# Last block of a windowed-attention layer: normalised values written in the row order of the output weights, transposed on the whole array, and a value halo of 128 columns

## The chip, the cores and the metric

The kernel runs on one core of a Trainium2 chip. The metric is the device time of the whole program in microseconds, as the median of several runs. A core has TensorE (PE; its weight loads are listed as PEld), VectorE (DVE), ScalarE (ACT), GpSimd (POOL) and SyncE (SP, which issues nearly all DMAs here). Each engine takes its instructions in the order of the program, and they wait for one another through semaphores. SBUF is the working memory of 128 partitions; PSUM holds what TensorE writes, in eight banks of 512 f32 values per partition.

## The reference

Four layers A, B, A, B act on x of 2048 positions and 512 features, all in bf16, with 32 heads of 16 features; both A layers share their weights, and so do both B layers. Layer B is the one that matters here:

```python
W, dil = 8, 2
qkv = (x @ wqkv).reshape(B, S, 3, H, Dh).transpose(2, 0, 3, 1, 4)
idx = pos[:, None] - (jnp.arange(W) * dil)[None, :]      # 8 positions back, every second one
logits = einsum("bhsd,bhswd->bhsw", q, k at idx) * Dh ** -0.5
attn = softmax(where(idx >= 0, logits, -1e9))
o = einsum("bhsw,bhswd->bhsd", attn, v at idx)
return o.transpose(0, 2, 1, 3).reshape(B, S, D) @ wo
```

Each layer's input is x normalised over its features, and its result is added to x. Layer A is a linear attention with softmax feature maps and has the same outer form.

## The kernel before, in words

The 2048 positions are cut into four blocks of 512 (b = 0 to 3), and each of the four layers runs over the blocks. L counts the pairs of layers, so that (L, b) = (1, 3) is the last block of the last layer B. A stage of a block is a list of steps per engine. The steps of all stages are put in one hand-made order, a long string of thread names (`_ORDER`); which engine copies a PSUM bank out (ACT or DVE) and which slot each tile takes are fixed by three more strings (`_CHOICE`, `_SLOTS`). Nothing is planned while the program runs: the order on each engine is the order of that string. The steps of several blocks are mixed, so that block (1, 2), by the general path, runs side by side with block (1, 3).

All blocks of layer B but the last take the general path: VectorE multiplies queries with shifted keys (`prod`, L1042) and weights with shifted values (`pav`, L1104), and TensorE sums over features or window positions with 0/1 matrices of 32 columns (L1049, L1113). The last block, (1, 3), takes another path, in four methods:

- `s_e1` projects keys and queries with features in partitions, and values with positions in partitions. For the window that reaches back, it also projects the last 64 positions of the block before: `hk` for keys, `hv` (L1192) for values, which makes a PSUM result of 64 partitions from 64 columns of stationary operand. `ehv` copies that to partitions 0 to 63 of plane 2 of a staging tile `Vs`, `vwh` (L1234) writes those 64 rows to a DRAM tile, together with the 512 rows of the block (`vwr`, L1231), and `vrd` (L1242) reads all of it back in 32-row groups with every second position, into the old space of a weight tile (`WA`) and a tile `Vx`. Each head has a 17th column of ones.
- `s_e2` makes scores for one of four tiles t of 128 positions (L1277), exponentials (L1298) and the mask (L1303).
- `s_e3` multiplies with the values (L1321, 32 or 8 columns each) into a PSUM tile `O` of two banks, which holds for each of e = 0 to 7 a run of 4 x 17 values, in 128: c = 0 to 3 and, for head 8c + e, 16 values and the sum of weights. The reciprocals of the sums are made on ACT (`ln`, `rd`, L1337 and L1340) as an f32 tile `r` of 8 x 4 (e by c). `nrm` (L1348, VectorE) multiplies and writes the bf16 tile `oB`, for tile t 512 columns in the order head, feature.
- `s_e4` transposes tile t with TensorE (`pt`, L1365), with matmuls whose moving operand is an identity with permuted columns: partitions hold positions sorted by even and odd, and `ident[:].rearrange("p (r q) -> p q r", r=2)` puts them in order again. ACT copies the PSUM bank to `oBT`, and `s_out` multiplies with the output weights (L542) and adds x (L555 on VectorE, or L545 on TensorE with L552 on ACT).

The output weights `WoB` are stored with rows sorted for both paths: chunk q, partition 32c + h holds row 16h + 4q + c. Before, `pt` makes this order: for each q and c, one matmul takes the 32 columns 4q + c, 4q + c + 16, and so on of `oB` as stationary operand and writes 32 partitions, at column tile 32c of the array.

After the last steps the program tests a flag (L1387 to L1415) that says whether the fast path held; the slow path behind it did not run.

Of the kernel before, what the change touches and what calls it, by code (L numbers as in the profile page):

```python
# [11 lines left out]
ALU = mybir.AluOpType  # L12
# [4 lines left out]
P = 128  # L17
NJ = 16
D = 512
H = 32  # L20
DH = 16
NW = 8
HALO = 14
NB = 4
# [8 lines left out]
DV = DH + 1  # L33
# [103 lines left out]
class _Fast:  # L137
# [1023 lines left out]
    def s_e1(self, L, b):  # L1161
        nc, add = self.nc, self.step
        st = "b1_%d%d" % (L, b)
        T = {}

        def mm(i, c):
            xnT = self.xnT["B%d" % L, b]
            T[i, c] = pp = self.ps()
            for k in range(NB):
                nc.tensor.matmul(pp[:], lhsT=self.WB[:, k, i * D + c * P:i * D + (c + 1) * P], rhs=xnT[:, :, k, :],  # L1170
                                 start=(k == 0), stop=(k == NB - 1))

        def hk():
            xp = self.xnT["B%d" % L, b - 1]
            T["hk"] = pp = self.ps()
            for c in range(NB):
                for k in range(NB):
                    nc.tensor.matmul(pp[:, c * 64:(c + 1) * 64], lhsT=self.WB[:, k, D + c * P:D + (c + 1) * P],
                                     rhs=xp[:, 3, k, 64:128], start=(k == 0), stop=(k == NB - 1))

        def mv(t):
            xnT = self.xnT["B%d" % L, b]
            T[2, t] = pp = self.ps()
            for k in range(NB):
                nc.tensor.matmul(pp[:], lhsT=xnT[:, t, k, :], rhs=self.WB[:, k, 2 * D:3 * D],
                                 start=(k == 0), stop=(k == NB - 1))

        def hv():
            xp = self.xnT["B%d" % L, b - 1]
            T["hv"] = pp = self.ps()  # L1190
            for k in range(NB):
                nc.tensor.matmul(pp[0:64, :], lhsT=xp[:, 3, k, 64:128], rhs=self.WB[:, k, 2 * D:3 * D],  # L1192
                                 start=(k == 0), stop=(k == NB - 1))

        def ehk(dve):
            self.copy(dve, self.kvT[:, 0:4 * 64], T["hk"][:, 0:4 * 64])

        def vs(u):
            if ("Vs", u) not in T:
                T["Vs", u] = self.med([3, H, DV], "Vs")  # L1200
            return T["Vs", u]

        def vones(u):
            nc.gpsimd.memset(vs(u)[:, :, :, DH:DV], 1.0)

        def ev(i, c, dve):
            if i == 2:
                self.copy(dve, vs(c // 2)[:, c % 2, :, 0:DH], T[i, c][:].rearrange("p (h d) -> p h d", d=DH))
                return
            if i == 1:  # L1210
                if (L, b) not in self.K:
                    self.K[L, b] = self.med([NB, TB], "K")
                dst = self.K[L, b]
            else:
                if i not in T:
                    T[i] = self.med([NB, TB], "Qs")
                dst = T[i]
            self.copy(dve, dst[:, c, :], T[i, c][:])

        def ehv(dve):  # L1220
            self.copy(dve, vs(0)[0:64, 2, :, 0:DH], T["hv"][0:64, :].rearrange("p (h d) -> p h d", d=DH))

        def qsc(g, i):
            lo = DH * g
            nc.sync.dma_start(out=self.Qbd[i][lo:lo + DH, :, g % 4, :], in_=T[0][lo:lo + DH, 2 * i:2 * i + 2, :])

        def vwr(u):
            if u == 0:
                self.VD[L, b] = self.dram.tile([64 + TB, H * DV], BF16, name="vd%d%d" % (L, b))
            dst = self.VD[L, b][64 + 256 * u:320 + 256 * u, :].rearrange("(t p) d -> p t d", p=P)  # L1230
            nc.sync.dma_start(out=dst, in_=vs(u)[:, 0:2, :, :].rearrange("p t h d -> p t (h d)"))  # L1231

        def vwh():
            nc.sync.dma_start(out=self.VD[L, b][0:64, :], in_=vs(0)[0:64, 2, :, :].rearrange("p h d -> p (h d)"))  # L1234

        def vrd(r, j0, j1, c):
            a = self.VD[L, b][64 * j0 + r:64 * j0 + r + 1, c * 8 * DV:(c + 1) * 8 * DV]
            n = H * DV
            src = bass.AP(a.tensor, a.offset, [[2 * n, 32], [64 * n, j1 - j0], [1, 8 * DV]])
            d = self.chunk(r, j0)[32 * c:32 * c + 32, c, :]  # L1240
            dst = bass.AP(d.tensor, d.offset, [list(d.ap[0]), [VCH, j1 - j0], [1, 8 * DV]])
            nc.sync.dma_start(out=dst, in_=src)  # L1242

        add(st + "h", "PE", hk)
        self.flex(st + "h", ehk)
        for i in (1, 0):
            for c in range(NB):
                add(st + "qk"[i], "PE", mm, i, c)
                self.flex(st + "qk"[i], ev, i, c)
        for i in range(2):  # L1250
            for g in range(8):
                add(st + "q", "SP", qsc, g, i)
        for u in range(2):
            add(st + "v", "POOL", vones, u)
        add(st + "h", "PE", hv)
        self.flex(st + "h", ehv)
        for t in range(4):
            add(st + "v", "PE", mv, t)
            self.flex(st + "v", ev, 2, t)
            if t % 2:  # L1260
                add(st + "v", "SP", vwr, t // 2)
            if t == 1:
                add(st + "v", "SP", vwh)
        for r, j0, j1 in ((0, 0, 9), (1, 0, 2), (1, 2, 9)):
            for c in range(NB):
                add(st + "v", "SP", vrd, r, j0, j1, c)
# [44 lines left out]
    def s_e3(self, L, b, t):  # L1311
        nc, add = self.nc, self.step
        st = "b3_%d%d" % (L, b)
        T = {}

        def pv(e, r, s, n, pos):
            j = 1 + 2 * t + s - (pos > 0)
            E = self.ET[t if s or not pos else (t - 1) % 4]
            ks = 2 * r + (s if not pos else 1 - s)
            q = 32 * (2 * r + s)  # L1320
            nc.tensor.matmul(T["O"][q:q + n, e, 0:NB * DV], lhsT=E[:, e // 4, ks, e % 4, pos:pos + n],  # L1321
                             rhs=self.chunk(r, j)[:, :, DV * e:DV * (e + 1)],
                             start=(e % 4 == 0 and pos == 0), stop=(pos > 0),
                             tile_position=(0, q), skip_group_check=True)

        def mo():
            T["O"] = self.pp().rearrange("p o (e x) -> p (o e) x", x=P)
            for pos, n in ((0, 32), (32, 8)):
                for e in range(8):
                    for r in range(2):  # L1330
                        for s in range(2):
                            pv(e, r, s, n, pos)

        def ln():
            T["r"] = self.sm([8, NB], "rdB")
            den = T["O"][:, :, 0:NB * DV].rearrange("p e (c d) -> p e c d", d=DV)[:, :, :, DH]
            nc.scalar.activation(out=T["r"][:], in_=den, func=ACT.Ln, bias=self.tiny_t[:, 0:1])  # L1337

        def rd():
            nc.scalar.activation(out=T["r"][:], in_=T["r"][:], func=ACT.Exp, scale=-1.0,  # L1340
                                 accum_out=self.stR[:, 7 + t:8 + t])

        def nrm():
            if (L, b) not in self.oB:
                self.oB[L, b] = self.med([4, D], "oB")
            num = T["O"][:, :, 0:NB * DV].rearrange("p e (c d) -> p e c d", d=DV)[:, :, :, 0:DH]
            out = self.oB[L, b][:, t, :].rearrange("p (c e d) -> p e c d", c=NB, d=DH)
            nc.vector.tensor_tensor(out=out, in0=num, in1=T["r"][:].unsqueeze(3).to_broadcast([P, 8, NB, DH]),  # L1348
                                    op=ALU.mult)

        add(st, "PE", mo)
        add(st, "ACT", ln)
        add(st, "ACT", rd)
        add(st, "DVE", nrm)

    def s_e4(self, L, b):
        nc, add = self.nc, self.step
        st, key = "b4_%d%d" % (L, b), "A%d" % (L + 1)
        U = {}

        def pt(t):
            U[t] = self.ps()
            for q in range(NB):
                for c in range(NB):
                    nc.tensor.matmul(U[t][32 * c:32 * c + 32, q * P:(q + 1) * P],  # L1365
                                     lhsT=self.oB[L, b][:, t, 4 * q + c::DH],
                                     rhs=self.ident[:].rearrange("p (r q) -> p q r", r=2), start=True, stop=True,
                                     tile_position=(0, 32 * c))

        def pe(t, dve):  # L1370
            if (key, b) not in self.oT:
# [145 lines left out]
class _Layout:  # L1517
# [6 lines left out]
    def add(self, name, nelem, nbuf=1):  # L1524
        self.regions[name] = (self.off, nelem, nbuf)
        self.off += nelem * nbuf
        return self
# [569 lines left out]
```

## Time and profile before

| | us |
|---|---|
| median of 3 runs (lowest, highest) | 322.31 (322.30, 322.36) |
| the profiled execution, its own time | 321.75 |
| its span, first to last instruction | 320.0 |
| PE busy | 307.5 |
| DVE busy | 295.9 |
| ACT busy | 274.9 |
| the four L1348 on DVE, together | 2.7 |
| the 64 L1365 on PE, together | 2.8 |
| the four L1192 on PE, together | 1.1 |

The page gives busy times for the whole span; the last 25 us are read from the timeline and from groups by shape. In a group's line stand line, engine, operation, tiles, shapes out and in, and count; behind the bar the busy time in us and the mean of one in ns; and behind the second bar the idle time ahead of them with what ended it. In a timeline's line stand start and length in us from the span's start; several instructions of a kind in a row are one line with a count. PE's matmuls overlap: the length of one, some 380 ns for 512 columns, is not the step from one to the next, some 216 ns.

### The profile page before, as it was taken

To read this page: it belongs to the slowest core of one execution; us is meant where nothing else is said; L and a number is where in the kernel's file an instruction comes from. 1 tells how busy PE (TensorE), PEld (TensorE's weight loads), DVE (VectorE), ACT (ScalarE), POOL (GpSimd) and SP (SyncE) were. 2 spreads that over 40 slices of the span, in tenths; PEclk is the share of its full clock that TensorE was granted. 3 is DMA by queue.
4 is the path that set the end of the run, shared out by engine and by line. 5 is a ranking of instruction groups with operands and counts; after the bars stand their busy time and mean duration, and the time that the engine had idled before them with its cause. 6 is when DMAs were issued, how large, how long until landed. Compare 5 with 4: busy or idle time off the path is not lost. (4 is left out here: it accounts for less than half of the span.)

```text
span 320.0 us, 8889 instructions
## 1 busy us (share of the span) xinstructions
PE 307.5 (96%) x3572; PEld 152.2 (48%) x3572; DVE 295.9 (92%) x458; ACT 274.9 (86%) x638; POOL 47.5 (15%) x64
## 2 busy tenths in 40 slices
PE   7999999899999999999999999879999999999993
PEld 3554456445454444444444455544444444444541
DVE  5999996998999999999999999599997999999993
ACT  4999999999898778999999999799999777698560
POOL 6000000000004121000000000041240744035000
PEclk9999999999999999999999999999999999999999
DMA  6977100005794979948994500014389855567733
GB/s 200 349 193 148 35 2 4 2 18 148 177 160 110 152 134 142 137 83 120 153 132 54 69 0 2 4 39 113 89 171 137 151 120 126 133 159 158 182 137 103
DMA packets 45789, 36.37 MB, mean 114 GB/s; under 512 B 30832, under 2 KB 41136, under 8 KB 45744
## 3 DMA queue, kind: packets, MB, share of 16 engines
q1 hardware_dynamic: 45216, 35.75, 55.8%
q8 instruction: 29, 0.48, 0.7%
q14 instruction: 16, 0.13, 0.2%
q10 hardware_dynamic: 528, 0.02, 0.1%
HBM read 11.13 MB, written 3.25 MB: 45 GB/s over the span
## 5 line engine op out<-in xcount | busy, mean ns | idle before, releaser
L950 PE MATMUL PS<-xnT,WB 128*128 128x512 bf16 x336 | 76.8, 379 | 0.1
L1042 DVE TENSOR_TENSOR prod<-QT,K 128x4096 bf16<-128x4096 bf16 x28 | 63.4, 2286 | 0.5 <-POOL K L976 0.5
L1104 DVE TENSOR_TENSOR pav<-PT,Vg 128x4096 bf16<-128x4096 bf16 (+1 forms) x29 | 62.9, 2215 | 0.2
L950 PEld LDWEIGHTS <-WB 128*128 128x128 bf16 x336 | 37.4, 114 | 36.3 <-issue 3.3
L728 ACT ACTIVATE Eq<-PS 128x512 bf16<-128x512 f32 x64 | 36.3, 619 | 0.0
L621 ACT ACTIVATE Ek<-PS 128x512 bf16<-128x512 f32 x64 | 35.1, 622 | 0.2 <-PE PS L615 0.2
L542 PEld LDWEIGHTS <-oT 128*128 128x128 bf16 x240 | 22.3, 98 | 27.1 <-issue 1.3
L720 PE MATMUL PS<-xnT,WA 128*128 128x512 bf16 x128 | 32.0, 380 | 0.5 <-DVE s L812 0.3
L562 ACT ACTIVATE sqd<-x 128x512 bf16<-128x512 bf16 x48 | 30.0, 635 | 2.2 <-DVE x L555 2.0
L555 DVE SCALAR_TENSOR_TENSOR x<-PS,x 128x512 bf16<-128x512 f32 x47 | 30.9, 684 | 1.0 <-PE PS L542 0.9
L627 PE MATMUL PS<-WA,xnT 128*128 128x512 bf16 x128 | 31.6, 379 | 0.0
L615 PE MATMUL PS<-WA,xnT 128*128 128x512 bf16 x128 | 30.7, 379 | 0.0
L204 ACT CAST oT<-PS 128x512 bf16<-128x512 f32 (+1 forms) x50 | 26.9, 599 | 4.3 <-PE PS L1113 2.6
L542 PE MATMUL PS<-WoA,oT 128*128 128x512 bf16 x128 | 29.8, 380 | 0.0
L542 PE MATMUL PS<-WoB,oT 128*128 128x512 bf16 x112 | 27.3, 379 | 0.0
L204 ACT CAST K<-PS 128x512 bf16<-128x512 f32 x30 | 17.3, 594 | 3.0 <-PE PS L950 1.9
L615 PEld LDWEIGHTS <-xnT 128*128 128x128 bf16 x128 | 12.4, 98 | 14.8 <-issue 0.4
L627 PEld LDWEIGHTS <-xnT 128*128 128x128 bf16 x128 | 12.2, 98 | 14.5 <-issue 0.4
L673 DVE TENSOR_TENSOR Ek<-Ek,rk 128x4096 bf16<-128x4096 bf16 (+1 forms) x10 | 18.6, 1860 | 0.4 <-ACT rk L668 0.4
L720 PEld LDWEIGHTS <-WA 128*128 128x128 bf16 x128 | 11.6, 98 | 14.6 <-issue 1.7
L465 DVE TENSOR_SCALAR xn<-x,rstd,nmr 128x512 bf16<-128x512 bf16 x48 | 17.9, 420 | 0.6
L204 ACT CAST V<-PS 128x512 bf16<-128x512 f32 x26 | 15.2, 596 | 2.6 <-PE PS L950 2.6
(164 smaller groups left out, 501.2 us busy)
## 6 DMA issues: line engine op xcount, KB each, us to landing
Vg<-V SPq DMA_DIRECT2D x112, 131.5 KB, 4.3
Prho<-rd SPq DMA_DIRECT2D x8, 512.0 KB, 5.7
x<-in_A_x_dram SPq DMA_DIRECT2D x3, 512.0 KB, 6.8
WB<-in_B_wqkv_dram SPq DMA_DIRECT2D x3, 512.0 KB, 9.9
out_dram<-x SPq DMA_DIRECT2D x6, 256.0 KB, 2.5
wraw<-in_A_wqkv_dram SPq DMA_DIRECT2D x4, 256.0 KB, 4.3
vd<-Vs SPq DMA_DIRECT2D x2, 272.0 KB, 3.0
x<-in_A_x_dram SPq DMA_DIRECT2D x4, 128.0 KB, 3.6
```

The source lines that it names most:

```text
L204: self.nc.scalar.copy(out=out, in_=in_)
L542: nc.tensor.matmul(y[:], lhsT=lh(t, c), rhs=Wo()[:, c, :], start=(c == 0), stop=(c == NB - 1 and not onpe))
L555: nc.vector.scalar_tensor_tensor(out=xb[:, t, :], in0=T[t][:], scalar=1.0, in1=xb[:, t, :], op0=ALU.mult, op1=ALU.add, **kw)
L562: nc.scalar.activation(out=sqd[:], in_=xb[:, t, :], func=ACT.Square, accum_out=T["ss"][:, t:t + 1])
L615: nc.tensor.matmul(pk[:], lhsT=xnT[:, t, k, :], rhs=self.WA[:, k, D:2 * D], start=(k == 0), stop=(k == NB - 1))
L621: nc.scalar.activation(out=T["E"][:, t, s, :], in_=T["k", t][:], func=ACT.Exp, scale=1.0 - 2.0 * s)
L627: nc.tensor.matmul(pv[:], lhsT=xnT[:, t, k, :], rhs=self.WA[:, k, 2 * D:3 * D], start=(k == 0), stop=(k == NB - 1))
L720: nc.tensor.matmul(pq[:], lhsT=self.WA[:, k, hb * P:(hb + 1) * P], rhs=xnT[:, :, k, :], start=(k == 0), stop=(k == NB - 1))
L728: nc.scalar.activation(out=self.Eq[L, b][s][:, :, hb, :], in_=T[hb][:].rearrange("p (t i) -> p t i", t=4), func=ACT.Exp, scale=1.0 - 2.0 * s)
L950: nc.tensor.matmul(pp[:], lhsT=self.WB[:, k, i * D + c:(i + 1) * D:NB], rhs=xnT[:, :, k, :], start=(k == 0), stop=(k == NB - 1))
L1042: nc.vector.tensor_tensor(out=pr[:], in0=QT[:, c:c + 1, :].to_broadcast([P, NW, TB]), in1=win, op=ALU.mult)
L1104: nc.vector.tensor_tensor(out=pv, in0=PT[:, :, lo:lo + n].unsqueeze(1).to_broadcast([P, NB, 2, n]), in1=vw, op=ALU.mult)
```

## The change

Three edits, all in the path of block (1, 3).

`hv` uses all 128 positions of the last tile of the block before as stationary operand, so that its PSUM result has 128 partitions, of which the last 64 are used. `ehv` copies partitions 64 to 127, to partitions 64 to 127 of `Vs`, and `vwh` writes to DRAM from there.

`nrm` walks its operands in the order feature d, then c, then e. It writes `oB` in the order d, c, e, which is 32d + h, so that columns 128q to 128q + 127 hold the features 4q + c of all heads in the order of the rows of `WoB`. The output is then dense; the PSUM input steps 128 f32 values from one element to the next, and the reciprocals step 4.

`pt` transposes four pieces of 128 dense columns with one matmul of 128 columns each, where it had sixteen of 32. The moving operand, the permuted identity, stays.

The order of steps, the tiles, the slots and the DMAs' sizes stay as they are. On TensorE 48 weight loads and 48 matmuls fall away; the other engines issue as many instructions as before.

```diff
@@ hv
-                nc.tensor.matmul(pp[0:64, :], lhsT=xp[:, 3, k, 64:128], rhs=self.WB[:, k, 2 * D:3 * D],
+                nc.tensor.matmul(pp[:], lhsT=xp[:, 3, k, :], rhs=self.WB[:, k, 2 * D:3 * D],
@@ ehv
-            self.copy(dve, vs(0)[0:64, 2, :, 0:DH], T["hv"][0:64, :].rearrange("p (h d) -> p h d", d=DH))
+            self.copy(dve, vs(0)[64:P, 2, :, 0:DH], T["hv"][64:P, :].rearrange("p (h d) -> p h d", d=DH))
@@ vwh
-            nc.sync.dma_start(out=self.VD[L, b][0:64, :], in_=vs(0)[0:64, 2, :, :].rearrange("p h d -> p (h d)"))
+            nc.sync.dma_start(out=self.VD[L, b][0:64, :], in_=vs(0)[64:P, 2, :, :].rearrange("p h d -> p (h d)"))
@@ nrm
-            num = T["O"][:, :, 0:NB * DV].rearrange("p e (c d) -> p e c d", d=DV)[:, :, :, 0:DH]
-            out = self.oB[L, b][:, t, :].rearrange("p (c e d) -> p e c d", c=NB, d=DH)
-            nc.vector.tensor_tensor(out=out, in0=num, in1=T["r"][:].unsqueeze(3).to_broadcast([P, 8, NB, DH]),
-                                    op=ALU.mult)
+            num = T["O"][:, :, 0:NB * DV].rearrange("p e (c d) -> p d c e", d=DV)[:, 0:DH]
+            out = self.oB[L, b][:, t, :].rearrange("p (d c e) -> p d c e", c=NB, d=DH)
+            rec = T["r"][:].rearrange("p e c -> p c e").unsqueeze(1).to_broadcast([P, DH, NB, 8])
+            nc.vector.tensor_tensor(out=out, in0=num, in1=rec, op=ALU.mult)
@@ pt
-            for q in range(NB):
-                for c in range(NB):
-                    nc.tensor.matmul(U[t][32 * c:32 * c + 32, q * P:(q + 1) * P],
-                                     lhsT=self.oB[L, b][:, t, 4 * q + c::DH],
-                                     rhs=self.ident[:].rearrange("p (r q) -> p q r", r=2), start=True, stop=True,
-                                     tile_position=(0, 32 * c))
+            for c in range(NB):
+                nc.tensor.matmul(U[t][:, c * P:(c + 1) * P], lhsT=self.oB[L, b][:, t, c * P:(c + 1) * P],
+                                 rhs=self.ident[:].rearrange("p (r q) -> p q r", r=2), start=True, stop=True)
```

## The prediction

> **What bounds the kernel where the change acts.** I read the page first, then the busy time by stretches, then the order of VectorE's and TensorE's instructions over the last 25 us, then the groups kept apart by shape. The page names no single bound: TensorE and VectorE are both above 90% of the span.
>
> ```profile
> PE 307.5 (96%) x3572; PEld 152.2 (48%) x3572; DVE 295.9 (92%) x458; ACT 274.9 (86%) x638; POOL 47.5 (15%) x64
> ```
>
> By stretches (busy us of PE, PEld, DVE, ACT, POOL; clock; DMA share), this stretch holds all four normalisations and all four transposes of the last block:
>
> ```profile
> 295.40:308.10 12.70, 12.54 (x258) 6.90 (x257) 12.66 (x18) 8.22 (x21) 0.00 (x0) 1.00 0.60 164
> ```
>
> VectorE is busy for 12.66 of 12.70 us, TensorE for 12.54. VectorE's instructions in order of time (start, length) show where the four L1348 stand:
>
> ```profile
> 295.47 1.28 DVE L1348 TENSOR_TENSOR oB<-PS,rdB 128x512 bf16<-128x512 f32 x2
> 296.67 0.81 DVE L1303 TENSOR_TENSOR et<-et,maskW 128x1280 bf16<-128x1280 bf16 x1
> ...
> 303.01 0.68 DVE L1348 TENSOR_TENSOR oB<-PS,rdB 128x512 bf16<-128x512 f32 x1
> 303.61 0.68 DVE L555 SCALAR_TENSOR_TENSOR x<-PS,x 128x512 bf16<-128x512 f32 x1
> 304.21 2.28 DVE L1104 TENSOR_TENSOR pav<-PT,Vg 128x4096 bf16<-128x4096 bf16 x1
> 306.43 0.69 DVE L1348 TENSOR_TENSOR oB<-PS,rdB 128x512 bf16<-128x512 f32 x1
> ```
>
> Each starts before or as its forerunner ends: there is no hole into which a longer L1348 could grow. Whatever one of them gains or loses, the fourth (306.43 to 307.12) feels four times. TensorE around it:
>
> ```profile
> 306.39 0.67 PE L1365 MATMUL PS<-ident,oB 128*32 128x128 bf16 x16
> 306.88 0.61 PE L1113 MATMUL PS<-pav,indAV 128*32 128x512 bf16 x8
> 307.31 0.67 PE L1365 MATMUL PS<-ident,oB 128*32 128x128 bf16 x16
> 307.91 1.90 PE L542 MATMUL PS<-WoB,oBT 128*128 128x512 bf16 x8
> 309.65 0.17 PE L1396 MATMUL PS<-okb,ones 128*128 128x4 bf16 x1
> 309.67 0.81 PE L542 MATMUL PS<-WoB,oT 128*128 128x512 bf16 x3
> 310.41 0.40 PE L1113 MATMUL PS<-pav,indAV 128*32 128x256 bf16 x8
> 311.29 0.40 PE L1113 MATMUL PS<-pav,indAV 128*32 128x256 bf16 x8 [0.48 <-ACT oT L204]
> ```
>
> The fourth transpose waits for the fourth L1348 (its weight load was idle 0.19 us for it, below). TensorE keeps its order, so L542, the flag matmul, the last L1113 and the closing L542 all queue behind that transpose. So the end is set by VectorE up to 307.12, then by the chain L1365, ACT's copy of oBT, L542, L1113, ACT, L1113, L542.
>
> ```profile
> 307.18 0.53 PEld L1365 LDWEIGHTS <-oB 128*32 128x32 bf16 x16 [0.19 <-DVE oB L1348]
> ```
>
> **Part 1, L1348.** Four instructions, still 512 values each, on the same waits. Each now walks its operands with the head index e innermost: the output becomes dense; the PSUM input steps 128 f32 = 512 bytes per element where it read runs of 16; the reciprocals in SBUF (f32, stored e by c) step 4 f32 = 16 bytes per element where each was held for 16. No row has exactly that. The nearest rows, by shape:
>
> ```profile
> L1348 DVE TENSOR_TENSOR oB<-PS,rdB 128x512 bf16<-128x512 f32 x4 | 2.7, 684 | 0.0
> L555 DVE SCALAR_TENSOR_TENSOR x<-PS,x 128x512 bf16<-128x512 f32 x47 | 30.9, 684 | 1.0 <-PE PS L542 0.9
> L267 DVE TENSOR_REDUCE indAV<-ident 128x32 bf16<-128x128 bf16 x1 | 0.4, 360 | 0.0
> L267 DVE TENSOR_REDUCE indQK<-ident 128x32 bf16<-128x128 bf16 x1 | 0.3, 276 | 0.0
> L1337 ACT ACTIVATE rdB<-PS,tiny_t 128x32 f32<-128x32 f32 x4 | 1.1, 288 | 1.5 <-PE PS L1321 1.4
> L1070 ACT ACTIVATE lnd<-PS,tiny_t 128x512 f32<-128x512 f32 x7 | 5.0, 716 | 0.9 <-PE PS L1065 0.9
> L204 ACT CAST oT<-PS 128x512 bf16<-128x512 f32 x48 | 26.2, 608 | 2.1 <-PE PS L923 0.9 <-DVE prod L1042 0.6 <-PE PS L1113 0.4
> L204 ACT CAST oT<-PS 128x256 bf16<-128x256 f32 x2 | 0.7, 373 | 2.2 <-PE PS L1113 2.2
> L812 DVE TENSOR_TENSOR s<-PS,rS 128x256 f32<-128x256 f32 x8 | 3.4, 420 | 1.6 <-ACT Eq L728 0.8 <-PE PS L804 0.5 <-ACT rS L743 0.3
> ```
>
> The output gives nothing back: L555 writes dense rows and takes the 684 ns of L1348, whose output is in 32-byte runs. For the inputs, the two L267 reductions are the same work (128 values of the identity to 32 sums of four), but indQK reads neighbours and indAV steps 32 bf16 = 64 bytes: 360 - 276 = 84 ns over 128 values, 0.66 ns each. That is VectorE itself, reading SBUF. For PSUM there is only ACT: L1337 takes a logarithm of 32 values in steps of 68 and 512 bytes in 288 ns. L1070 takes one of 512 dense values in 716; a dense value costs ACT (608 - 373)/256 = 0.92 ns by the two L204 rows, so 32 dense ones would take 716 - 480 x 0.92 = 274. The 14 ns left are 0.44 ns per value, or 0.23 us over 512: less than SBUF's, and read beside it, so I let it hide there and price the reciprocals' step alone: 512 x 0.66 = 0.34 us per L1348, 1.35 us for four.
>
> Bounds: below, nothing (if reading ahead hides the step). Above, the ratio that TensorE shows when it streams the identity in steps of 128 bytes (L1365) against dense (L481):
>
> ```profile
> 228.68 1.06 PE L481 MATMUL PS<-ident,xn 128*128 128x128 bf16 x16
> L481 PE MATMUL PS<-ident,xn x80: 219/219/229, 7.3 to 229.5; 128*128 128x128 bf16 x80
> L1365 PE MATMUL PS<-ident,oB x64: 282/285/337, 296.7 to 307.7; 128*32 128x128 bf16 x64
> ```
>
> Sixteen dense ones start (1.06 - 0.219)/15 = 56 ns apart. L1365's sixteen, four side by side, start in (0.67 - 0.285)/3 = 128 ns steps: 2.3 times as long. A dense value costs VectorE (684 - 420)/256 = 1.03 ns between L1348 and L812, 0.53 us for 512. A doubling is +0.53 us each, 2.1 us in all; at 2.3 times, 0.69 each and 2.8. I take 0.34, because L267 is the same engine and memory.
>
> [...]
>
> **Part 2, the transposes.** Sixty-four matmuls and loads of 32 columns become sixteen of 128. The load is not the price: 98 ns for 128 dense columns against 139 for 32 stepped ones.
>
> ```profile
> L1365 PEld LDWEIGHTS <-oB 128*32 128x32 bf16 x64 | 2.2, 139 | 0.5 <-DVE oB L1348 0.2
> L542 PEld LDWEIGHTS <-oBT 128*128 128x128 bf16 x16 | 1.5, 98 | 1.9 <-ACT oBT L204 0.5
> L950 PEld LDWEIGHTS <-WB 128*128 128x128 bf16 x123 | 13.8, 114 | 12.7 <-issue 0.5
> ```
>
> But before, four matmuls ran side by side, and the moving operand keeps its stepped order. Four full ones in turn at 128 ns take the 0.51 us that four groups of four took. So TensorE gains about 0 per tile; at the dense 56 ns it would be 4 x (0.128 - 0.056) = 0.29 us each. (L950's loads step 8 bytes: 114 ns against 98, nearly free. 16 bytes lies between that and the 32 of L1365.)
>
> New are changes of the array's shape. L1113 and L1321 use 32 columns; the transposes did too. In the rows above the three L542 start (0.81 - 0.38)/2 = 0.215 apart, the last at 310.10, yet L1113 starts at 310.41, 0.31 later: 0.09 us for the change. Tiles 0 and 2 stand between 32-column work and gain two changes each; tiles 1 and 3 stand ahead of L542 and only move one. [...] Tile 0's 0.18 us is covered, since the next matmuls wait for VectorE's L1303 (0.43 us idle). Tile 2's delays L1113 at 306.88, and tile 3 then pays entry too: about 0.3 us on TensorE at 307.31, were VectorE no later. With L1348 longer, VectorE reaches that point 1.35 us later and TensorE only 2 x 0.34 + 0.3 = 1.0 us later (it waited for VectorE at 297.54), so the changes hide in the wait.
>
> ```profile
> 297.54 0.58 PEld L1321 LDWEIGHTS <-et 128*32 128x32 bf16 x64 [0.43 <-DVE et L1303]
> ```
>
> **Part 3, the halo.** Four L1192 matmuls get 128 columns instead of 64; the load falls from 109 to 98 ns, the stream of 512 stays, and the copy still moves 64 partitions. I cost it at nothing: some 0.04 us of loads under matmuls. The write of 64 rows issues at 279.10 in the same place on SP, and such writes landed in 2.0 to 3.2 us; the readers issue from 283.17. Half a microsecond more, from the other partitions, would still not be waited for; what stands behind it on SP (L1231, L1011) does not wait for its landing.
>
> ```profile
> L1192 PEld LDWEIGHTS <-xnT 128*64 128x64 bf16 x4 | 0.4, 109 | 0.6 <-issue 0.4
> 279.10 0.52 SPq L1234 DMA_DIRECT2D vd<-Vs  x1
> 283.17 4.66 SPq L1242 DMA_DIRECT2D WA<-vd  x8
> DMA to landing us min/median/max: 2.0/2.7/3.2
> ```
>
> ```profile
> 308.06 0.60 ACT L204 CAST oBT<-PS 128x512 bf16<-128x512 f32 x1
> ```
>
> **Sum.** 4 x 0.34 = 1.35 us on VectorE, 0 on the transposes behind it (0.09 saved as L542 no longer changes shape, lost again since the last four L542 of oBT wait for ACT's copy, above, which waits for the fourth transpose), 0 for the halo. Against the profiled run's own 321.75 us (span 320.0 and 1.75 around it): 323.1. The median of the runs is 322.31, 0.56 above that run, so 323.65; forecast 323.6.
>
> **Rivals.**
> First, the step costs VectorE nothing or little (under 0.16 us each). For: ACT's L1337 shows little excess from PSUM, and 16 bytes is a smaller step than L267's 64. Against: L267. Then the shape changes decide: about +0.27 us at tile 3, 322.6, within 0.2% (0.64 us, about what a measurement here can tell from no change). Chance 0.28.
> Second, the step doubles the time per element, or PSUM's 512-byte step adds its own: +0.53 to 0.69 us each, 324.4 to 325.1. For: TensorE's 2.3. Against: L267's (1.03 + 0.66)/1.03 = 1.6 on VectorE. Chance 0.20.
> Third, faster: full-array matmuls stream the stepped identity at the dense 56 ns, so that tiles 2 and 3 each give back 0.29 us on TensorE and the loads some more, with L1348 unchanged. Place: 306.39 to 307.91. Price: 2 x 0.29 less the 0.3 of shape changes, 322.0; it passes 0.2% only if the changes too cost nothing and ACT's copy, which starts at 308.06, moves up with it. Against: the 219 and 285 ns of one matmul differ by the step, not by the width. Chance of more than 0.2%: 0.05.
> The forecast (0.16 to 0.5 us each) has 0.47; its own range is 322.95 to 324.3.
>
> **Numbers.** Slower: 0.47 + 0.20 = 0.67; same 0.28; faster 0.05. The range goes from the first rival's time less 0.2 (322.4) to the middle of the second (324.8); about 1 in 10 is left on either side.
>
> **What would show it.** L1348 at 0.95 to 1.1 us instead of 0.684, still back to back on VectorE; sixteen transposes near 285 ns, some 125 apart; the fourth one starting 1.2 to 1.5 us after 307.31; halo copy and landing as before. Wrong if L1348 stays near 0.68 (then the tail moves by tenths, by TensorE alone), or if it passes 1.3 us, or if the transposes start 56 ns apart.

## The result, and the profile after

The changed kernel takes 322.92 us (median of 22 runs, 322.46 to 323.54), the kernel before 322.01 us (median of 22, 321.52 to 322.50; the first three runs, shown above, lie in the upper part of that). The ratio is 1.0027, 95% interval 1.0020 to 1.0033: slower by 0.9 us, between 0.6 and 1.1. The profiled execution of the changed kernel took 323.16 us, with a span of 321.4.

The normalisation moved from L1348 to L1349 and the transposes from L1365 to L1364. The groups by shape of the changed kernel, which answer to those shown for the kernel before (busy us, mean ns of one, idle time before):

```profile
L1349 DVE TENSOR_TENSOR oB<-PS,rdB 128x512 bf16<-128x512 f32 x4 | 4.1, 1047 | 0.0
L1364 PE MATMUL PS<-ident,oB 128*128 128x128 bf16 x16 | 2.6, 287 | 0.3 <-DVE oB L1349 0.3
L1364 PEld LDWEIGHTS <-oB 128*128 128x128 bf16 x16 | 1.2, 98 | 1.9 <-DVE oB L1349 1.2 <-issue 0.4
L1192 PEld LDWEIGHTS <-xnT 128*128 128x128 bf16 x4 | 0.4, 98 | 0.5
```

One normalisation takes 1047 ns instead of 684, still with no idle time ahead of it. VectorE in order of time, after:

```profile
295.56 2.01 DVE L1349 TENSOR_TENSOR oB<-PS,rdB 128x512 bf16<-128x512 f32 x2
297.48 0.83 DVE L1303 TENSOR_TENSOR et<-et,maskW 128x1280 bf16<-128x1280 bf16 x1
...
303.82 1.04 DVE L1349 TENSOR_TENSOR oB<-PS,rdB 128x512 bf16<-128x512 f32 x1
304.77 0.69 DVE L555 SCALAR_TENSOR_TENSOR x<-PS,x 128x512 bf16<-128x512 f32 x1
305.38 2.29 DVE L1104 TENSOR_TENSOR pav<-PT,Vg 128x4096 bf16<-128x4096 bf16 x1
307.57 1.05 DVE L1349 TENSOR_TENSOR oB<-PS,rdB 128x512 bf16<-128x512 f32 x1
```

The first normalisation starts at nearly the same time (295.56 against 295.47), the fourth ends at 308.62 instead of 307.12. TensorE around it, after:

```profile
307.14 0.66 PE L1364 MATMUL PS<-ident,oB 128*128 128x128 bf16 x4
307.74 0.61 PE L1113 MATMUL PS<-pav,indAV 128*32 128x512 bf16 x8
308.68 0.66 PE L1364 MATMUL PS<-ident,oB 128*128 128x128 bf16 x4 [0.33 <-DVE oB L1349]
309.18 1.89 PE L542 MATMUL PS<-WoB,oBT 128*128 128x512 bf16 x8
...
311.67 0.40 PE L1113 MATMUL PS<-pav,indAV 128*32 128x256 bf16 x8
312.55 0.40 PE L1113 MATMUL PS<-pav,indAV 128*32 128x256 bf16 x8 [0.47 <-ACT oT L204]
```

TensorE now waits 0.33 us for the fourth normalisation and starts its transposes 1.37 us later than before (308.68 against 307.31); L542 behind them is 1.27 us later. The last group of each timeline on VectorE, before and after, ends the arithmetic:

```profile
312.70 2.70 DVE L555 SCALAR_TENSOR_TENSOR x<-PS,x 128x512 bf16<-128x512 f32 x4 [0.55 <-PE PS L542]
```

```profile
313.96 2.70 DVE L555 SCALAR_TENSOR_TENSOR x<-PS,x 128x512 bf16<-128x512 f32 x4 [0.31 <-PE PS L542]
```

From the start of the first normalisation to the end of this group it is 312.70 + 2.70 - 295.47 = 19.93 us before and 313.96 + 2.70 - 295.56 = 21.10 after: 1.17 us. This stretch, called the tail below, is the part of the program that the normalisation and the transposes touch. The start of the first normalisation itself wandered from 295.31 to 296.37 us among the profiles, in kernels that differ up to there only in the halo, in a small early copy or fill on GpSimd and in the order in which ACT writes the reciprocals, and so the tail says more than two spans do. It is still the tail of one execution each.

### The profile page after: what moved, and what is told of

It is laid out like the page before. It is cut to its first block, busy times and chain, and to the rows that moved or that the text cites. A ratio compares the mean times of both kernels' runs of the same rounds, so it can differ in the third digit from the quotient of the medians.

```text
span 321.4 us, 8793 instructions
## 1 busy us (share of the span) xinstructions
PE 307.6 (96%) x3524; PEld 151.4 (47%) x3524; DVE 297.2 (92%) x458; ACT 275.0 (86%) x638; POOL 47.5 (15%) x64
## 5 line engine op out<-in xcount | busy, mean ns | idle before, releaser
L542 PEld LDWEIGHTS <-oT 128*128 128x128 bf16 x240 | 22.4, 98 | 26.9 <-issue 1.1
L542 PE MATMUL PS<-WoA,oT 128*128 128x512 bf16 x128 | 29.8, 380 | 0.0
L542 PE MATMUL PS<-WoB,oT 128*128 128x512 bf16 x112 | 27.3, 380 | 0.0
```

The lines of the kernel that those rows point to most:

```text
L542: nc.tensor.matmul(y[:], lhsT=lh(t, c), rhs=Wo()[:, c, :], start=(c == 0), stop=(c == NB - 1 and not onpe))
```

## The experiments

Intervals are of the ratio to the kernel before on the same chip. A ratio of 1.001 is 0.32 us.

**Which operand costs: reciprocals dense, PSUM still stepped.**

```diff
-            T["r"] = self.sm([8, NB], "rdB")
+            T["r"] = self.sm([NB, 8], "rdB")
...
-            nc.scalar.activation(out=T["r"][:], in_=den, ...)
+            nc.scalar.activation(out=T["r"][:].rearrange("p c e -> p e c"), in_=den, ...)
...
-            rec = T["r"][:].rearrange("p e c -> p c e").unsqueeze(1).to_broadcast([P, DH, NB, 8])
+            rec = T["r"][:].unsqueeze(1).to_broadcast([P, DH, NB, 8])
```

> The changed kernel, with the reciprocals stored c by e, so that the normalisation reads them one f32 after the other; its PSUM input keeps the step of 512 bytes. If the SBUF step is the cost (my theory): the normalisation falls from 1.05 back to about 0.68 us, the fourth one ends some 1.45 us earlier, and the time is that of the kernel before plus the shape changes on TensorE, about +0.3 us (ratio 1.000 to 1.0015). If PSUM's step is the cost (rival): it stays at 1.05 us and the ratio near 1.0027. If both cost and hide behind each other: it stays near 1.05 too, and the run that steps SBUF alone also shows 1.05.

Ratio 0.9997 (0.9986 to 1.0008), a little under the 1.000 to 1.0015 expected: the loss is gone. The group of the normalisation and that of the logarithm which now writes in steps:

```profile
L1349 DVE TENSOR_TENSOR oB<-PS,rdB 128x512 bf16<-128x512 f32 x4 | 2.6, 682 | 0.0
L1337 ACT ACTIVATE rdB<-PS,tiny_t 128x32 f32<-128x32 f32 x4 | 1.3, 317 | 1.7 <-PE PS L1321 1.6
```

The normalisation is back at 682 ns, against 684 in the kernel before, though seven of every eight of its 512 PSUM values still lie 512 bytes from the last. So the step in PSUM costs VectorE nothing that this shows. The step moved to the writing of 32 values on ACT, where it costs 29 ns (288 to 317). VectorE in this profile:

```profile
296.01 1.28 DVE L1349 TENSOR_TENSOR oB<-PS,rdB 128x512 bf16<-128x512 f32 x2
...
298.17 0.69 DVE L1077 TENSOR_TENSOR PT<-E,rden 128x1024 bf16<-128x1024 bf16 x1
...
307.18 0.68 DVE L1349 TENSOR_TENSOR oB<-PS,rdB 128x512 bf16<-128x512 f32 x1
...
313.55 2.70 DVE L555 SCALAR_TENSOR_TENSOR x<-PS,x 128x512 bf16<-128x512 f32 x4 [0.67 <-PE PS L542]
```

Its tail is 313.55 + 2.70 - 296.01 = 20.24 us, 0.31 over the kernel before. Of that, 0.21 lie ahead of the fourth normalisation (307.18 - 296.01 = 11.17 us against 306.43 - 295.47 = 10.96) and 0.10 behind it. The interval of the ratio ends at 0.26 us, so the whole 0.31 is not what the runs lose.

**The same step alone, and two others.** In the kernel before, PSUM is read in runs and the second operand comes from a table of ones in SBUF; the division by the sums is left out:

```diff
+                self.rstep = self.PHI[:].rearrange("p a b c -> p (a b c)").bitcast(F32)[:, 0:64]
+                nc.gpsimd.memset(self.rstep, 1.0)
...
-            nc.vector.tensor_tensor(out=out, in0=num, in1=T["r"][:].unsqueeze(3).to_broadcast([P, 8, NB, DH]),
+            nc.vector.tensor_tensor(out=out, in0=num, in1=self.rstep[:, 0:64:4].unsqueeze(1).unsqueeze(1).to_broadcast([P, 8, NB, DH]),
```

Steps of 2 and 8 f32 are made in the same way, with tables of 32 and 128 values.

> The kernel before (PSUM read in dense runs of 16, output in runs of 16), but its normalisation reads the second operand in steps of 4 f32 (16 bytes) from a table of ones; the normalisation by the sums is left out, so the output is another. If the SBUF step alone costs: 1.0 to 1.1 us instead of 0.684. If PSUM's step is the cost: 0.68 us. If it needs both: between.

> The kernel before, its normalisation reading the second operand from a table of ones in steps of 2 f32 (8 bytes); the normalisation by the sums is left out. [...]

> The same with steps of 8 f32 (32 bytes); the normalisation by the sums is left out. [...]

The groups, for steps of 16, 8 and 32 bytes:

```profile
L1350 DVE TENSOR_TENSOR oB<-PS,PHI 128x512 bf16<-128x512 f32 x4 | 4.2, 1082 | 0.0
```

```profile
L1350 DVE TENSOR_TENSOR oB<-PS,PHI 128x512 bf16<-128x512 f32 x4 | 2.7, 691 | 0.0
```

```profile
L1350 DVE TENSOR_TENSOR oB<-PS,PHI 128x512 bf16<-128x512 f32 x4 | 4.3, 1087 | 0.0
```

The step in SBUF alone does all of it. 8 bytes is free (691 ns against 684), 16 costs 0.4 us (1082 ns), and 32 costs no more than 16 (1087 ns). The price of 16 bytes is 0.7 to 0.8 ns per value: (1047 - 684)/512 = 0.71 in the changed kernel, (1082 - 684)/512 = 0.78 here. Why 16 bytes costs and 8 does not, no run shows. The times, one run each, go the same way: 321.94 us for 8 bytes, 323.51 and 323.74 for 16 and 32. The tails are 19.92, 21.40 and 21.41 us, against 19.93 before: four times 0.4 is 1.6, and 1.5 of it comes out at the end.

**The transposes back in 32 columns**, on the new order of oB:

```diff
-            for c in range(NB):
-                nc.tensor.matmul(U[t][:, c * P:(c + 1) * P], lhsT=self.oB[L, b][:, t, c * P:(c + 1) * P], ...)
+            for q in range(NB):
+                for c in range(NB):
+                    lo = q * P + 32 * c
+                    nc.tensor.matmul(U[t][32 * c:32 * c + 32, q * P:(q + 1) * P],
+                                     lhsT=self.oB[L, b][:, t, lo:lo + 32], ..., tile_position=(0, 32 * c))
```

> The changed kernel, with the transposes back in sixteen matmuls of 32 columns (now dense columns of oB), so without the added changes of array shape. If VectorE decides (my theory): the normalisation stays at 1.05 us and the time within 0.15 us of the changed kernel, ratio 1.002 to 1.0035; it may be a tenth slower, since the fourth transpose is again followed by a change of shape. If the shape changes cost what the result shows (rival): the 0.9 us go, ratio under 1.001.

Ratio 1.0031 (1.0019 to 1.0043), like the changed kernel's: the whole array and the changes of its shape are not the loss. In the profile of this run TensorE comes from the fourth transposes to L542 as follows:

```profile
308.76 0.67 PE L1366 MATMUL PS<-ident,oB 128*32 128x128 bf16 x16 [0.36 <-DVE oB L1349]
309.59 1.67 PE L542 MATMUL PS<-WoB,oBT 128*128 128x512 bf16 x7 [0.16 <-issue]
```

One L542 of eight has no record here, so the 309.59 says nothing; but the tail is 314.15 + 2.70 - 295.63 = 21.22 us, 0.12 longer than in the changed kernel, with a normalisation of 1060 ns. The expected tenth is about what this one profile shows.

**The permuted identity made dense**, by one copy on GpSimd, in the kernel before and in the changed one; then with the dense reciprocals, and with 32 columns as well:

```diff
+                self.identP = self.PHI[:].rearrange("p a b c -> p (a b c)")[:, 0:P]
+                nc.gpsimd.tensor_copy(out=self.identP.rearrange("p (q r) -> p q r", r=2),
+                                      in_=self.ident[:].rearrange("p (r q) -> p q r", r=2))
...
-                                 rhs=self.ident[:].rearrange("p (r q) -> p q r", r=2), start=True, stop=True)
+                                 rhs=self.identP, start=True, stop=True)
```

> The kernel before, with the permuted identity made dense once (one copy on GpSimd, long before). The moving operand of the transposes is then read without steps. If the step in the moving operand sets the pace (my theory): groups of four start 56 instead of 122 ns apart, matmul 219 instead of 285 ns; the fourth transpose ends 0.25 us sooner, of which some 0.1 to 0.25 us reach the end: ratio 0.999 to 1.0. If the stepped weight loads (139 ns) set the pace (rival): the groups stay over 100 ns apart and nothing moves.

> The changed kernel, with the permuted identity made dense once. If the step of the moving operand kept the whole-array transposes from being faster (my theory): they start 56 ns apart instead of 122, the fourth ends 0.26 us sooner, and the time falls by 0.1 to 0.3 us under the changed kernel (ratio 1.0015 to 1.0025); the normalisation stays 1.05. If width sets the pace: 122 ns still, ratio 1.0027.

> The changed kernel with the identity dense and the reciprocals stored c by e. If the SBUF step was VectorE's cost: normalisation 0.68 us, transposes 56 ns apart, and the shape changes paid from the transposes' gain: ratio 0.9985 to 1.0005. If PSUM's step was the cost: normalisation 1.05 us, and the same as the run with the dense identity alone.

> The changed kernel with the reciprocals stored c by e, the permuted identity made dense, and the transposes in sixteen matmuls of 32 dense columns: no stepped operand in SBUF is left on VectorE or TensorE here, and no shape changes are added. Normalisation 0.68 us, groups of transposes 56 to 60 ns apart, ratio 0.9985 to 1.0; by the theory that only VectorE's step counted and TensorE's part is hidden: 1.0.

| | ratio (95%) | tail, us | normalisation, ns |
|---|---|---|---|
| before, identity dense | 0.9996 (0.9986 to 1.0006) | 19.56 | 681 |
| changed, identity dense | 1.0032 (1.0020 to 1.0044) | 21.02 | 1042 |
| changed, identity and reciprocals dense | 0.9993 (0.9984 to 1.0001) | 19.98 | 686 |
| the same with 32 columns | 0.9996 (0.9985 to 1.0007) | 19.80 | 688 |

TensorE's transposes in the second of these (whole array, identity dense):

```profile
307.54 0.40 PE L1367 MATMUL PS<-PHI,oB 128*128 128x128 bf16 x4
...
309.35 0.40 PE L1367 MATMUL PS<-PHI,oB 128*128 128x128 bf16 x4 [0.35 <-DVE oB L1352]
```

```profile
L1367 PE MATMUL PS<-PHI,oB 128*128 128x128 bf16 x16 | 1.6, 222 | 0.0
```

(The last line is that of the run with both dense.) One takes 222 ns instead of 287, and four start (0.40 - 0.222)/3 = 0.06 us apart instead of (0.66 - 0.287)/3 = 0.12. So it is the step of the moving operand, some 128 bytes, and not the width, that sets the pace of these transposes: some (0.12 - 0.06)/128 us, or 0.5 ns, more per moving value. No other step was run on TensorE, so it is not shown from which step on it costs there. In the kernel before the same edit brings sixteen from 0.67 to between 0.41 and 0.48 us, 233 ns each where 219 were expected.

The ratio of the changed kernel with a dense identity, 1.0032, is a miss: I expected a gain of 0.1 to 0.3 us and none came out. In its profile the way from the start of the fourth normalisation to the end did shorten, from 313.96 + 2.70 - 307.57 = 9.09 us to 314.36 + 2.71 - 308.23 = 8.84, but the way from the first normalisation to the fourth was 0.17 us longer, and the interval is too wide for a quarter of a microsecond.

None of the four is shown to beat the kernel before: three of the intervals hold 1, and that of the changed kernel with a dense identity lies above it. Both with dense reciprocals are faster than the changed kernel, whose interval starts at 1.0020.

**The halo, alone and undone.** The three lines of the diff on `hv`, `ehv` and `vwh`, put into the kernel before, and taken out of the changed one.

> The kernel before, with the value halo of 128 columns alone. My theory: no change, ratio 0.999 to 1.001, weight loads of L1192 98 ns instead of 109, matmuls 379 ns as before. Rival: the halo write from partitions 64 to 127 lands later and the readers wait, then a ratio over 1.0015.

> The changed kernel, with the value halo as before (64 columns, partitions 0 to 63). If the halo is worth nothing (my theory): the ratio of the changed kernel, 1.002 to 1.0035. If the wait of 1.1 us that L1321 shows in the changed kernel for the read-back of the values comes from the halo's new partitions and reaches the end (rival): ratio under 1.001.

Ratios 1.0000 (0.9988 to 1.0013) and 1.0029 (1.0017 to 1.0041). The halo is worth nothing either way, as costed. The wait of 1.1 us of L1321 for the read-back of values, which I had seen in the changed kernel, stands in the run without the halo too, and is missing in the run with the halo alone, so it is not the halo's (the view of waits of the run without the halo: us in total, times, longest):

```profile
PEld L1321 <- DMA Vx<-vd: 1.0, 1, 1.0
```

In the run with the halo alone another row is of use. VectorE after the first two normalisations:

```profile
296.37 1.52 DVE L1348 TENSOR_TENSOR oB<-PS,rdB 128x512 bf16<-128x512 f32 x2
297.80 0.81 DVE L1303 TENSOR_TENSOR et<-et,maskW 128x1280 bf16<-128x1280 bf16 x1
299.01 0.69 DVE L1077 TENSOR_TENSOR PT<-E,rden 128x1024 bf16<-128x1024 bf16 x1 [0.40 <-ACT rden L1072]
...
314.21 2.70 DVE L555 SCALAR_TENSOR_TENSOR x<-PS,x 128x512 bf16<-128x512 f32 x4 [0.48 <-PE PS L542]
```

Two normalisations cover 1.52 us here instead of 1.28, and L1077 waits another 0.40 for ACT's `rden`. It starts 299.01 - 296.37 = 2.64 us after the first normalisation, where in the kernel before it started 1.93 after it (297.40). So this execution has holes of 0.7 us on VectorE, and its tail is 314.21 + 2.70 - 296.37 = 20.54 us, although the kernel does the same work on VectorE as the kernel before.

What makes the hole is when ACT finishes `rden` (L1072). The line before, after, and in the run with the halo alone:

```profile
296.40 0.63 ACT L1072 ACTIVATE rden<-lnd 128x512 bf16<-128x512 f32 x1
```

```profile
297.34 0.63 ACT L1072 ACTIVATE rden<-lnd 128x512 bf16<-128x512 f32 x1
```

```profile
298.25 0.63 ACT L1072 ACTIVATE rden<-lnd 128x512 bf16<-128x512 f32 x1
```

Counted from the start of the first normalisation these end at 1.56, 2.41 and 2.51 us. In the last of these profiles L1077, behind its gap, starts 0.13 us after that end (299.01 against 298.25 + 0.63). In the changed kernel's profile it starts at 2.66 us (298.22) with no gap ahead of it. An estimate from these numbers: with short normalisations it would have started at 2.41 + 0.13 = 2.54 us in that execution, so that there the first two long ones delayed it by some 0.1 us and not by 0.7. The change did not make `rden` late: ACT had waited 1.40 us for TensorE's L1321 before 293.92, ahead of the first normalisation, and had no pause from there to `rden`.

## Why the prediction was right or wrong

*The price of L1348.* Right, and by the reason given: 0.34 us foreseen from the two L267 reductions, 0.363 measured (1047 - 684). Of the two steps it was the reciprocals' that cost. PSUM's cost nothing, so the 0.23 us that the prediction let hide beside it, from ACT's rows, were not there at all. The doubt whether 16 bytes is more like 8 or 32 is settled: it is like 32 (691, 1082 and 1087 ns).

*Where it comes out.* Right: VectorE stayed full (busy for 12.70 us of the 12.70 from 295.40 to 308.10), the fourth normalisation ended 1.41 us later counted from the first, and the fourth transposes started 1.37 us after 307.31, within the 1.2 to 1.5 foreseen. One reading behind it was off. The prediction has the fourth transposes of the kernel before wait for the fourth normalisation, but only their weight load did. The matmuls start at 307.31, just as the two rounds of four L1113 ahead of them are through (306.88 + 2 x 0.216). In the changed kernel the transposes start 0.06 us after the end of the normalisation, which in the kernel before would have been 307.18. So the first 0.13 us of any delay there were free.

*The transposes.* Right in pace: 287 ns each, 0.12 us apart, 0 gained per tile. Wrong in one small term: I let the 0.09 us saved behind the fourth transposes be lost again on ACT's copy. It stayed saved: L542 came 0.50 us after the start of the transposes (309.18 - 308.68) where it had come 0.60 after (307.91 - 307.31). With the 0.13 us ahead of them, which I had not counted, that makes 1.41 - 0.13 - 0.10 = 1.18 us, and 1.17 were measured.

*The shape changes.* Right that they hide in the wait for VectorE, which was 0.33 us at the fourth transposes. With dense reciprocals that cover is gone, and TensorE shows the price:

```profile
307.73 0.61 PE L1113 MATMUL PS<-pav,indAV 128*32 128x512 bf16 x8
308.28 0.66 PE L1364 MATMUL PS<-ident,oB 128*128 128x128 bf16 x4
```

The transposes start 0.55 us after the L1113 ahead of them instead of 0.43 (307.31 - 306.88), 0.12 for the added change where 0.09 was foreseen. Counted from the fourth normalisation they start 0.22 us later than in the kernel before (308.28 - 307.18 = 1.10 against 0.88), where the prediction had some 0.3; about half of it is won back behind them, and 0.10 is left at the end. The other 0.21 us of this tail goes with a gap ahead of L1077, which starts 2.16 us after the first normalisation (298.17 - 296.01) instead of 1.93. A wait of L1077 for `rden` stands as well in profiles without the added changes: 0.40 us in the run with the halo alone, 0.20 in the last run of the table. So the 0.27 us of the first rival did not come out at the end, as far as one profile tells.

*The halo.* Right: 98 instead of 109 ns per load, its write landed 2.0 us after issue in both kernels, and nothing shows in the time.

*The size.* 1.3 us forecast, 0.9 measured (0.6 to 1.1), on a kernel before that turned out at 322.01 instead of 322.31. In the order of the sum: 1.35 as forecast, 1.45 as the instruction measured, 1.41 at the end of the fourth normalisation, less 0.23 at the two ends of the fourth transposes, is about the 1.17 of the profiled pair. What lies between 1.17 and 0.9 has a likely cause, the prediction's "no hole", which it read off one execution in which `rden` came early. Where `rden` comes late, part of a longer normalisation falls into the hole: against the tail of the run with the halo alone, 20.54 us, the changed kernel's 21.10 is longer by only 0.56. The 0.9 us of the medians lie between 0.56 and 1.17. That a mix of such executions makes up the medians is not shown, since no run tells how often each comes.

*The rivals.* The first (no cost of the step) and the third (dense pace on the whole array) fell. So did the second: the time per element did not double (0.363 us more, against 0.53 to 0.69), and PSUM's step added nothing of its own.

## What to carry to other kernels

Read each operand's innermost step in bytes before reordering a loop on VectorE: in SBUF, 512 f32 values 8 bytes apart were read at full pace (691 ns against 684) and 16 bytes apart took 0.36 to 0.40 us more, while a 512-byte step in PSUM was free (682 ns). Look at a tiny operand that is broadcast too: here all of the cost, 0.363 us per normalisation, was the step in 32 reciprocals per partition. Store it in the order in which it will be read, and let the engine that writes its few values pay for the step (29 ns on ACT against 363 ns on VectorE, four times each). And where VectorE had no holes, the price of one instruction times its count was nearly what the last of them was late (1.45 us by the count, 1.41 measured); but that there are no holes takes more than one profile to say, as the 0.7 us in the run with the halo alone show.

## What was not expected of the hardware

The step in PSUM cost VectorE nothing (682 against 684 ns), where I had let up to 0.23 us hide behind SBUF's. On TensorE a moving operand that steps some 128 bytes from one value to the next was about twice as slow as a dense one (0.12 against 0.06 us for 128 columns), whether four tiles of 32 columns ran side by side or one of 128 alone, so that the two ways of transposing took the same time for one stepped identity (0.66 us for four, 0.67 for sixteen), and the same shorter time for a dense one (0.40 us for four or for sixteen in the two last runs of the table):

```profile
305.80 0.40 PE L1369 MATMUL PS<-PHI,oB 128*32 128x128 bf16 x16
```
